# Scores and query projections on two concurrent 64-row PE tiles, one run per two head pairs, values and output projection in 128-row mode

## The chip, the cores and the metric

One core of one Trainium2 chip. The metric is the device time of one execution in microseconds (us), lower is better; the runs of the kernel before in this study lie between 947.7 and 952.4 us. A profile shows one execution. PE is the matrix engine (PEld its weight loads), DVE the vector engine, ACT the engine of the exponentials, POOL and SP the engines whose queues start DMAs here.

## The reference, cut to what matters

```python
x = A_x                                   # 2048 x 640
xn = layernorm(x)
q = xn @ wq                               # 32 heads of 192
k, v = last 512 rows of the caches, per head
s = softmax(q k^T * 192**-0.5) v @ wo     # attention, output projection
h = sigmoid(xn @ w_gate) * (xn @ w_up)
out = x + s * silu(h @ w_down)
```

## The kernel before

The gating part (h, w_down) comes first and takes 168 us. Attention then goes through 8 groups of two head pairs, and in each group through 4 blocks of 512 query rows. A step is one head pair in one block: scores, output projection of an earlier block, query projection of the next step, values. A head has 192 = 128 + 64 contraction rows, so a pair has four full 128-row score matmuls per half of the keys, and 64-row ones that two heads can run at once on the upper and lower half of the PE array:

```python
def stage_q(s, hp):                       # query projection, 128-row mode
    for j in range(PC):                   # 3 tiles of 128 columns per pair
        q_ps = bank()
        for c in range(NCD):              # 5 chunks of 128 rows
            nc.tensor.matmul(q_ps, lhsT=wqp[:, c, j*P:(j+1)*P], rhs=xnT[s][:, c, :], ...)
        # copied to SBUF by ACT (j == 1) or DVE

def full(S_ps, c, i, start):              # 128 rows
    nc.tensor.matmul(S_ps, lhsT=kT[:, c*PC + 2*i, :], rhs=qT[2*i][:], ...)
def half(S_ps, c, i, start):              # 64 rows, head i on half i of the array
    r = slice(64*i, 64*i + 64)
    nc.tensor.matmul(S_ps, lhsT=kT[r, c*PC + 1, :], rhs=qT[1][r, :], ...)

for u in u0: full(*u, True)               # 4 full
for u in u0: half(*u, False)              # 4 half   } one run of eight
for u in u1: half(*u, True)               # 4 half   } in 64-row mode
for u in u1: full(*u, False)              # 4 full
# ... (exponentials by ACT, one per 512 columns)

# a step: scores, two tiles of output projection (stage_wo), stage_q of the next, values
```

Each pair's values are normalised by DVE into o_st and transposed by a DMA into oT, which the output projection reads two steps later.

The softmax here doesn't subtract the row's maximum and nothing guards it: scores larger than these inputs give would overflow.

## Time and profile before

Median 949.78 us; the profiled execution spans 946.2 us. The head of the page of the kernel before: busy time and share of the span per engine, and the granted PE clock in 40 slices.

```profile
span 946.2 us, 16135 instructions
...
PE 933.0 (99%) x6554; PEld 533.6 (56%) x6554; DVE 443.3 (47%) x927; ACT 345.8 (37%) x654; POOL 160.6 (17%) x206
...
PEclk9999999999999999999999999999999999999999
```

The waits of PE in the kernel before (engine and line, what it waited for, us in total, times, longest):

```profile
PE ps_all L219 <- ACT xnT_89 L238: 3.2, 4, 0.8
PE ps_all L208 <- DVE warm L205: 1.5, 1, 1.5
PE ps_all L339 <- DVE qT_1587 L330: 0.6, 1, 0.6
PE ps_all L414 <- DMA oT<-o_st: 0.3, 1, 0.3
```

PE is busy 99% and waits for others for 5.6 us in all, so its time is the sum of the intervals from one matmul's start to the next. A step takes 12.02 us (402.89 to 414.91 below, the same score matmul of two successive steps). The scores of one step, from the timeline (start us, duration us, engine, line, operation, count, idle before):

```profile
402.89 0.38 PE L339 MATMUL ps_all<-qT_3908,kT 128*128 128x512 bf16 x1
...
403.10 0.38 PE L339 MATMUL ps_all<-qT_3922,kT 128*128 128x512 bf16 x1
403.41 0.55 PEld L346 LDWEIGHTS <-kT 64*128 64x128 bf16 x8 [0.42 <-issue]
403.41 1.04 PE L346 MATMUL ps_all<-qT_3915,kT 64*128 64x512 bf16 x8
...
404.38 0.39 PE L339 MATMUL ps_all<-qT_3908,kT 128*128 128x512 bf16 x1
404.61 0.38 PE L339 MATMUL ps_all<-qT_3922,kT 128*128 128x512 bf16 x1
...
414.91 0.38 PE L339 MATMUL ps_all<-qT_4028,kT 128*128 128x512 bf16 x1
```

Read starts, not durations: a 512-column matmul takes 0.38 us but the next starts 0.216 us later. From 403.10 to 403.41, into the 64-row matmuls, it is 0.31; the eight take 0.97 to the next start, where four pairs at 0.216 would take 0.864. That is about 0.2 us per step that moves no data: the two changes of tile mode.

### The profile page before, as it was taken

How to read it: one execution, taken by the hardware profiler on the slowest of the kernel's cores; microseconds unless marked ns; L12 is line 12 of the kernel's file. 1: busy time of each engine (PE TensorE's matmuls, PEld its weight loads, DVE VectorE, ACT ScalarE, POOL GpSimd, SP SyncE). 2: the span in 40 equal slices, each digit the busy share in tenths (PEclk: the TensorE clock that was granted, in tenths of full speed). 3: DMA queues.
4: the chain of work that ended last, by engine and by line, in shares of the span. 5: the costliest groups of instructions: out<-in, count | busy, mean ns of one | idle time of the engine just before them, and what ended most of it. 6: DMA issues, size and time to landing. Idle time of an engine off the chain costs nothing. (4 is left out here: it accounts for less than half of the span.)

```text
span 946.2 us, 16135 instructions
## 1 busy us (share of the span) xinstructions
PE 933.0 (99%) x6554; PEld 533.6 (56%) x6554; DVE 443.3 (47%) x927; ACT 345.8 (37%) x654; POOL 160.6 (17%) x206
## 2 busy tenths in 40 slices
PE   7999999999999999999999999999999999999996
PEld 5445455555555555555555555555555555555554
DVE  4842322444444444444444444444444444444566
ACT  3322222443333333333333333333333333333330
POOL 7100000400200020001100110011001106666100
PEclk9999999999999999999999999999999999999999
DMA  9940000651473157325631463147314833333433
GB/s 292 232 91 29 1 29 15 209 95 31 100 100 84 35 88 114 85 34 88 114 84 34 89 113 84 35 76 126 85 34 56 145 90 82 87 87 88 120 87 103
DMA packets 149258, 84.41 MB, mean 89 GB/s; under 512 B 136480, under 2 KB 139040, under 8 KB 149184
## 3 DMA queue, kind: packets, MB, share of 16 engines
q1 hardware_dynamic: 136384, 36.71, 23.1%
q0 software_dynamic: 12800, 46.67, 18.4%
q8 instruction: 51, 0.84, 0.4%
q14 instruction: 23, 0.19, 0.1%
HBM read 44.70 MB, written 5.24 MB: 53 GB/s over the span
## 5 line engine op out<-in xcount | busy, mean ns | idle before, releaser
L414 PE MATMUL ps_all<-wo_g,oT 128*128 128x512 bf16 (+1 forms) x1536 | 219.0, 299 | 0.3 <-DMA oT<-o_st 0.3
L414 PEld LDWEIGHTS <-oT 128*128 128x128 bf16 x1536 | 120.6, 98 | 98.3 <-DMA oT<-o_st 0.7
L322 PEld LDWEIGHTS <-wqp 128*128 128x128 bf16 x960 | 91.4, 98 | 106.1
L388 DVE TENSOR_TENSOR o_st<-ps_all,rden 128x384 bf16<-128x384 f32 x256 | 142.8, 558 | 8.9
L339 PEld LDWEIGHTS <-kT 128*128 128x128 bf16 x512 | 43.7, 97 | 58.7 <-issue 28.2
L270 DVE TENSOR_TENSOR hT_sb<-ps_all,sig_sb 128x512 bf16<-128x512 f32 x48 | 32.6, 682 | 52.7 <-PE ps_all L264 45.3
L322 PE MATMUL ps_all<-xnT_90,wqp 128*128 128x512 bf16 x240 | 54.4, 379 | 0.0
L322 PE MATMUL ps_all<-xnT_89,wqp 128*128 128x512 bf16 x240 | 54.4, 379 | 0.0
L322 PE MATMUL ps_all<-xnT_91,wqp 128*128 128x512 bf16 x240 | 54.4, 379 | 0.0
L322 PE MATMUL ps_all<-xnT_92,wqp 128*128 128x512 bf16 x240 | 54.4, 379 | 0.0
L279 PE MATMUL ps_all<-wd_sb,hT_sb 128*128 128x512 bf16 (+1 forms) x384 | 52.8, 299 | 0.0
L269 ACT ACTIVATE sig_sb<-ps_all 128x512 bf16<-128x512 f32 x48 | 28.6, 597 | 66.0 <-PE ps_all L264 52.2
L346 PEld LDWEIGHTS <-kT 64*128 64x128 bf16 x512 | 19.6, 94 | 42.4 <-issue 27.1
L387 DVE RECIPROCAL rden<-ps_all 128x2 f32<-128x2 f32 x256 | 41.6, 163 | 3.5
L279 PEld LDWEIGHTS <-hT_sb 128*128 128x128 bf16 x384 | 29.7, 98 | 23.1
L264 PEld LDWEIGHTS <-wu_sb 128*128 128x128 bf16 x225 | 22.0, 98 | 26.5
L264 PEld LDWEIGHTS <-wg_sb 128*128 128x128 bf16 x225 | 21.9, 98 | 26.2 <-issue 0.4
L313 POOL DMA_DIRECT2D wo_g<-in_A_wo_dram x8 | 6.9, 859 | 173.0 <-PE ps_all L414 170.8
L292 POOL DMA_DIRECT2D gB_d<-gB_sb x16 | 8.7, 545 | 128.7 <-DVE gB_sb L287 128.7
L287 DVE TENSOR_TENSOR gB_sb<-ps_all,sg 128x640 bf16<-128x640 f32 x16 | 13.2, 825 | 34.6 <-ACT sg L286 34.6
L128 POOL DMA_DIRECT2D v_sb_93<-in_A_v_cache_dram x4 | 3.0, 749 | 154.3 <-PE ps_all L381 153.5
L128 POOL DMA_DIRECT2D v_sb_101<-in_A_v_cache_dram x4 | 3.0, 749 | 153.2 <-PE ps_all L381 153.2
(924 smaller groups left out, 1527.1 us busy)
## 6 DMA issues: line engine op xcount, KB each, us to landing
wqp<-in_A_wq_dram POOLq DMA_DIRECT2D x16, 480.0 KB, 8.5
wo_g<-in_A_wo_dram POOLq DMA_DIRECT2D x8, 960.0 KB, 5.8
k_sb<-in_A_k_cache_dram POOLq DMA_DIRECT2D x32, 192.0 KB, 5.6
gBa_sb<-gB_d POOLq DMA_DIRECT2D x32, 160.0 KB, 2.7
gB_d<-gB_sb POOLq DMA_DIRECT2D x16, 160.0 KB, 2.1
xa_sb<-in_A_x_dram POOLq DMA_DIRECT2D x16, 160.0 KB, 2.9
out_dram<-o_sb SPq DMA_DIRECT2D x16, 160.0 KB, 2.4
wd_sb<-in_B_w_down_dram POOLq DMA_DIRECT2D x1, 1920.0 KB, 17.1
```

The costliest lines, as they stand in the source:

```text
L264: nc.tensor.matmul(ps, lhsT=w[:, c, f * P:(f + 1) * P], rhs=xnT[s][:, c, :], start=(c == 0), stop=(c == NCD - 1),)
L269: nc.scalar.activation(sig_sb[:], g_ps, AF.Sigmoid)
L270: nc.vector.tensor_tensor(hT_sb[:, f, :], u_ps, sig_sb[:], ALU.mult)
L279: nc.tensor.matmul(oB_ps[:, d0:d0 + dsz], lhsT=hT_sb[:, f, q * P:(q + 1) * P], rhs=wd_sb[:, f, d0:d0 + dsz], start=(f == 0), stop=(f == NF ...
L287: nc.vector.tensor_tensor(gB_sb[:], oB_ps[:, 0:D], sg[:], ALU.mult)
L292: nc.gpsimd.dma_start(gB_d[t * P:(t + 1) * P, :], gB_sb[:])
L322: nc.tensor.matmul(q_ps, lhsT=wqp[:, c, j * P:(j + 1) * P], rhs=xnT[s][:, c, :], start=(c == 0), stop=(c == NCD - 1),)
L339: nc.tensor.matmul(S_ps, lhsT=kT[:, c * PC + 2 * i, :], rhs=qT[2 * i][:], start=start, stop=not start,)
L346: nc.tensor.matmul(S_ps, lhsT=kT[r, c * PC + 1, :], rhs=qT[1][r, :], start=start, stop=not start,)
L387: nc.vector.reciprocal(rden[:], o_ps[:, :, DH:DH + 1])
L388: nc.vector.tensor_tensor(o_st[:, qp * 2:qp * 2 + 2, i * DH:(i + 1) * DH], o_ps[:, :, 0:DH], rden[:].to_broadcast([P, 2, DH]), ALU.mult,)
L414: nc.tensor.matmul(oA[:, d0:d0 + dsz], lhsT=oTs[pp][:, q * PC + j, :], rhs=wo_t[g][:, cc, d0:d0 + dsz], start=(cc == 0), stop=(cc == n - 1),)
```

## The change

Its intent: all scores and the query projections are cut into 64-row pieces that run as pairs on the two halves of the array, for two head pairs of a block in one run of 11.7 us. Values and output projection follow in 128-row mode. So PE changes its mode twice per two head pairs instead of four times. That needs q with a head per half of the partitions, weights of wq in pieces of 64 x 64 columns (six loads per pair with runs of 128 bytes instead of one load with runs of 768 bytes), k in pieces of 64 columns, and a second copy xnS of the transposed x with its halves swapped. PSUM is handed out as four double banks; one exponential covers two banks. The last output tile is finished in two halves of 320 columns.

```diff
-    def bank(): ...                      # eight single banks
+    ring = list(range(4))                # four double banks
+    def bank2():
+        b = ring.pop(0); ring.append(b)
+        return ps_all[:, 2 * b:2 * b + 2, :]
# ... load_pair
-        wqp = wq_pool.tile([P, NCD, 2 * DH], BF16, name="wqp")
-        nc.gpsimd.dma_start(wqp[:], wq_r[:, :, hp * 2 * DH:(hp + 1) * 2 * DH])
+        for j in range(PC):
+            jj = (hp % G) * PC + j
+            r = HI if jj % 2 else LO
+            for i in range(2):
+                d0 = (2 * hp + i) * DH + j * HF
+                nc.gpsimd.dma_start(
+                    wqp[r, jj // 2, :, i, :],
+                    wq_r[:, :, :, d0:d0 + HF].rearrange("p c h n -> p (c h) n"),
+                )
# ... stage_q, per two of a block's six tiles
+        for c in range(NCD):
+            for h in range(2):
+                for b, r in enumerate((LO, HI)):
+                    x = xnT if b == h else xnS
+                    nc.tensor.matmul(
+                        ps[:, b, :], lhsT=wq_t[g][r, u, 2 * c + h].rearrange("p i e -> p (i e)"),
+                        rhs=x[s][r, c, :], ...)
+        nc.vector.tensor_copy(qT_t[n][:, 2 * u:2 * u + 2, :], ps)
# ... stage_s, one chunk of keys of one pair
+        for j in range(PC):
+            for b, r in enumerate((LO, HI)):
+                nc.tensor.matmul(
+                    ps[:, b, :], lhsT=kT[r, c * PC + j, :], rhs=qT[r, pp * PC + j, :], ...)
+        nc.scalar.activation(E_t[n, pp][:, c, :, :], ps, AF.Exp, scale=scale_qk)
# ... the last output tile
+            h = D // 2
+            for d0, d1 in ((0, h), (h, D)):
+                wo_mm(...); finish(oA, gB_sb, t, d0, d1)
# ... the order of a block
+        for k, (pp, c) in enumerate(todo):           # 8 score units
+            stage_s(n, pp, c)
+            if k % 2 == 1 and k // 2 < G * PC // 2 and n < last:
+                stage_q(n + 1, k // 2)               # 3 projection units
+        for k, u in enumerate(pv):                   # 4 value units,
+            stage_pv(*u)                             # an output tile after each
+            stage_wo(*wo[k])
```

More of the change, by code (lines that the diff above doesn't have):

```diff
@@ L55 @@
     NG = NPAIR // G
-    HOLD = 2
     NWARM = 12
@@ L73, with flat @@
     ps_all = psum.tile([P, 8, 512], F32, name="ps_all")
-    ring = list(range(8))
-    def bank():
+    ring = list(range(4))
+    def bank2():
         b = ring.pop(0)
         ring.append(b)
-        return ps_all[:, b, :]
-    def bank2():
-        pos = {b: i for i, b in enumerate(ring)}
-        b = min(range(7), key=lambda b: max(pos[b], pos[b + 1]))
-        for x in (b, b + 1):
-            ring.remove(x)
-            ring.append(x)
-        return ps_all[:, b:b + 2, :].rearrange("p b n -> p (b n)")
+        return ps_all[:, 2 * b:2 * b + 2, :]
+    def flat(ps):
+        return ps.rearrange("p b n -> p (b n)")
     ident = const.tile([P, P], BF16, name="ident")
@@ L98 @@
     xnt_pool = ctx.enter_context(tc.tile_pool(name="xnt_pool", bufs=1, **rs))
-    wq_pool = ctx.enter_context(tc.tile_pool(name="wq_pool", bufs=2 * G, **rs))
+    wq_pool = ctx.enter_context(tc.tile_pool(name="wq_pool", bufs=2, **rs))
     k_pool = ctx.enter_context(tc.tile_pool(name="k_pool", bufs=2, **rs))
@@ L102 @@
     v_pool = ctx.enter_context(tc.tile_pool(name="v_pool", bufs=1, **rs))
+    HF = 64
+    LO, HI = slice(0, HF), slice(HF, P)
+    xnS = [xnt_pool.tile([P, NCD, 512], BF16, name=f"xnS{s}") for s in range(NST)]
     xnT = [xnt_pool.tile([P, NCD, 512], BF16, name=f"xnT{s}") for s in range(NST)]
@@ L111 @@
         v_tiles.append(vt)
-    wq_r = A_wq.rearrange("(c p) n -> p c n", p=P)
+    wq_r = A_wq.rearrange("(c h p) n -> p c h n", h=2, p=HF)
     wo_r = A_wo.rearrange("(c p) d -> p c d", p=P)
@@ L118, in load_pair @@
     def load_pair(hp):
-        k_sb = k_pool.tile([P, KC, 2, DH], BF16, name="k_sb")
+        k_sb = k_pool.tile([P, KC * PC, 2, 64], BF16, name="k_sb")
         vv = []
@@ L124, in load_pair @@
                 k_sb[:, :, i, :],
-                A_k_cache[0, hk, Sk - W:Sk, :].rearrange("(p j) d -> p j d", j=KC),
+                A_k_cache[0, hk, Sk - W:Sk, :].rearrange("(p k) (j e) -> p (k j) e", k=KC, j=PC),
             )
@@ L133, in load_pair @@
         v_t[hp] = vv
-        wqp = wq_pool.tile([P, NCD, 2 * DH], BF16, name="wqp")
-        nc.gpsimd.dma_start(wqp[:], wq_r[:, :, hp * 2 * DH:(hp + 1) * 2 * DH])
-        wq_t[hp] = wqp
+        if hp % G == 0:
+            wq_t[hp // G] = wq_pool.tile([P, G * PC // 2, NCD * 2, 2, HF], BF16, name="wqp")
+        wqp = wq_t[hp // G]
+        for j in range(PC):
[7 more added lines that the diff above has]
+                )
         kT = kt_pool.tile([P, KC * PC, P], BF16, name="kT")
-        nc.sync.dma_start_transpose(kT[:], k_sb[:].rearrange("p j e d -> p (j e d)"))
+        nc.sync.dma_start_transpose(kT[:], k_sb[:].rearrange("p k i e -> p (k i e)"))
         kT_t[hp] = kT
@@ L205 @@
         nc.vector.memset(warm[:], 0.0)
-        w_ps = bank()
+        pT_banks = bank2()
+        w_ps = pT_banks[:, 0, :]
         for _ in range(NWARM):
             nc.tensor.matmul(w_ps, lhsT=warm[:, 0:P], rhs=warm[:], start=True, stop=True)
-        gu_first = [
-            [bank() for _ in range(2)] for _ in range(FA)
-        ]
+        gu_first = [bank2() for _ in range(FA)]
         def first_mm(q, f):
             r = slice(q * P, (q + 1) * P)
-            for ps, w in zip(gu_first[f], (wg_sb, wu_sb)):
+            for i, w in enumerate((wg_sb, wu_sb)):
                 for c in range(NCD):
                     nc.tensor.matmul(
-                        ps[:, r], lhsT=w[:, c, f * P:(f + 1) * P], rhs=xnT[0][:, c, r],
+                        gu_first[f][:, i, r], lhsT=w[:, c, f * P:(f + 1) * P], rhs=xnT[0][:, c, r],
                         start=(c == 0), stop=(c == NCD - 1),
                     )
-        pT_banks = [w_ps, bank()]
         ln_stats(0)
@@ L234 @@
             xn = ln_apply(q)
-            pT = pT_banks[q % 2][:, 0:NCD * P // 2].bitcast(BF16).rearrange("p (c n) -> p c n", c=NCD)
+            pT = pT_banks[:, q % 2, 0:NCD * P // 2].bitcast(BF16).rearrange("p (c n) -> p c n", c=NCD)
             for c in range(NCD):
@@ L258 @@
                 if s == 0 and f < FA:
-                    g_ps, u_ps = gu_first[f]
+                    gu = gu_first[f]
                 else:
-                    g_ps, u_ps = bank(), bank()
-                    for ps, w in ((g_ps, wg_sb), (u_ps, wu_sb)):
+                    gu = bank2()
+                    for i, w in enumerate((wg_sb, wu_sb)):
                         for c in range(NCD):
                             nc.tensor.matmul(
-                                ps, lhsT=w[:, c, f * P:(f + 1) * P], rhs=xnT[s][:, c, :],
+                                gu[:, i, :], lhsT=w[:, c, f * P:(f + 1) * P], rhs=xnT[s][:, c, :],
                                 start=(c == 0), stop=(c == NCD - 1),
@@ L268 @@
                 sig_sb = bwork.tile([P, 512], BF16, name="sig_sb")
-                nc.scalar.activation(sig_sb[:], g_ps, AF.Sigmoid)
-                nc.vector.tensor_tensor(hT_sb[:, f, :], u_ps, sig_sb[:], ALU.mult)
+                nc.scalar.activation(sig_sb[:], gu[:, 0, :], AF.Sigmoid)
+                nc.vector.tensor_tensor(hT_sb[:, f, :], gu[:, 1, :], sig_sb[:], ALU.mult)
                 if s == 0 and TQ + f < NST * TQ:
@@ L275 @@
             for q in range(TQ):
-                oB_ps = bank2()
+                oB_ps = flat(bank2())
                 for f in range(NF):
@@ L292 @@
                 nc.gpsimd.dma_start(gB_d[t * P:(t + 1) * P, :], gB_sb[:])
+            if s == 0:
+                for ss in range(NST):
+                    nc.sync.dma_start(xnS[ss][LO], xnT[ss][HI])
+                    nc.sync.dma_start(xnS[ss][HI], xnT[ss][LO])
     acc_pool = ctx.enter_context(tc.tile_pool(name="acc_pool", bufs=1))
@@ L298 @@
     e_pool = ctx.enter_context(tc.tile_pool(name="e_pool", bufs=2))
-    ost_pool = ctx.enter_context(tc.tile_pool(name="ost_pool", bufs=3))
-    oT_pool = ctx.enter_context(tc.tile_pool(name="oT_pool", bufs=3 * G))
+    ost_pool = ctx.enter_context(tc.tile_pool(name="ost_pool", bufs=2))
+    oT_pool = ctx.enter_context(tc.tile_pool(name="oT_pool", bufs=2 * G))
     small = ctx.enter_context(tc.tile_pool(name="small", bufs=8))
@@ L314, in load_group, with stage_q @@
         wo_t[g] = wo_g
-    def stage_q(s, hp):
-        wqp = wq_t[hp]
-        qT = []
+    def stage_q(n, u):
+        g, s = blocks[n]
+        if u == 0:
+            qT_t[n] = qT_pool.tile([P, G * PC, 512], BF16, name="qT")
+        ps = bank2()
+        for c in range(NCD):
[4 more added lines that the diff above has]
+                        ps[:, b, :], lhsT=wq_t[g][r, u, 2 * c + h].rearrange("p i e -> p (i e)"),
+                        rhs=x[s][r, c, :],
+                        start=(c == 0 and h == 0), stop=(c == NCD - 1 and h == 1),
+                    )
+        nc.vector.tensor_copy(qT_t[n][:, 2 * u:2 * u + 2, :], ps)
@@ L319, in stage_q, with stage_s @@
+    def stage_s(n, pp, c):
+        g, s = blocks[n]
+        kT, qT = kT_t[g * G + pp], qT_t[n]
+        if c == 0:
+            E_t[n, pp] = e_pool.tile([P, KC, 2, 512], BF16, name="E")
+        ps = bank2()
         for j in range(PC):
-            q_ps = bank()
-            for c in range(NCD):
+            for b, r in enumerate((LO, HI)):
                 nc.tensor.matmul(
-                    q_ps, lhsT=wqp[:, c, j * P:(j + 1) * P], rhs=xnT[s][:, c, :],
-                    start=(c == 0), stop=(c == NCD - 1),
-                )
@@ L326, in stage_q @@
-            qT_sb = qT_pool.tile([P, 512], BF16, name=f"qT{j}", tag=f"qT{j}")
-            if j == 1:
-                nc.scalar.activation(qT_sb[:], q_ps, AF.Copy)
-            else:
-                nc.vector.tensor_copy(qT_sb[:], q_ps)
-            qT.append(qT_sb)
-        return qT
-    def stage_s(hp, qT):
-        kT = kT_t[hp]
-        E = [e_pool.tile([P, KC, 512], BF16, name=f"E{i}", tag=f"E{i}") for i in range(2)]
-        def full(S_ps, c, i, start):
-            nc.tensor.matmul(
-                S_ps, lhsT=kT[:, c * PC + 2 * i, :], rhs=qT[2 * i][:],
-                start=start, stop=not start,
-            )
-        def half(S_ps, c, i, start):
-            r = slice(64 * i, 64 * i + 64)
-            nc.tensor.matmul(
-                S_ps, lhsT=kT[r, c * PC + 1, :], rhs=qT[1][r, :],
-                start=start, stop=not start,
-            )
-        def units(cs):
-            return [(bank(), c, i) for c in cs for i in range(2)]
-        def exps(us):
-            for S_ps, c, i in us:
-                nc.scalar.activation(E[i][:, c, :], S_ps, AF.Exp, scale=scale_qk)
-        u0 = units(range(0, KC // 2))
-        for u in u0:
-            full(*u, True)
-        for u in u0:
-            half(*u, False)
-        exps(u0)
-        u1 = units(range(KC // 2, KC))
-        for u in u1:
-            half(*u, True)
-        for u in u1:
-            full(*u, False)
-        exps(u1)
-        return E
@@ L372, in stage_pv @@
-    def stage_pv(hp, E):
-        o_st = ost_pool.tile([P, TQ, 2 * DH], BF16, name="o_st")
-        for i in range(2):
-            vt = v_t[hp][i]
-            for qp in range(TQ // 2):
-                o_ps = bank()[:, 0:2 * OW].rearrange("p (i n) -> p i n", i=2)
-                for ii in range(2):
-                    q = qp * 2 + ii
-                    for c in range(KC):
-                        nc.tensor.matmul(
-                            o_ps[:, ii, 0:DH + 1], lhsT=E[i][:, c, q * P:(q + 1) * P],
-                            rhs=vt[:, c, 0:DH + 1],
-                            start=(c == 0), stop=(c == KC - 1),
-                        )
-                rden = small.tile([P, 2, 1], F32, name="rden")
-                nc.vector.reciprocal(rden[:], o_ps[:, :, DH:DH + 1])
-                nc.vector.tensor_tensor(
-                    o_st[:, qp * 2:qp * 2 + 2, i * DH:(i + 1) * DH],
-                    o_ps[:, :, 0:DH], rden[:].to_broadcast([P, 2, DH]), ALU.mult,
-                )
-        oT = oT_pool.tile([P, TQ * PC, P], BF16, name="oT")
-        nc.sync.dma_start_transpose(oT[:], o_st[:].rearrange("p q d -> p (q d)"))
-        return oT
+                    ps[:, b, :], lhsT=kT[r, c * PC + j, :], rhs=qT[r, pp * PC + j, :],
@@ new lines, in stage_s, with stage_pv @@
+                    start=(j == 0), stop=(j == PC - 1),
+                )
+        nc.scalar.activation(E_t[n, pp][:, c, :, :], ps, AF.Exp, scale=scale_qk)
+    def stage_pv(n, pp, i):
+        g, s = blocks[n]
+        hp = g * G + pp
+        if i == 0:
+            ost_t[0] = ost_pool.tile([P, TQ, 2 * DH], BF16, name="o_st")
+        o_st = ost_t[0]
+        E, vt = E_t[n, pp], v_t[hp][i]
+        o_ps = bank2()[:, :, 0:2 * OW].rearrange("p b (i n) -> p b i n", i=2)
+        for q in range(TQ):
+            for c in range(KC):
+                nc.tensor.matmul(
+                    o_ps[:, q // 2, q % 2, 0:DH + 1], lhsT=E[:, c, i, q * P:(q + 1) * P],
+                    rhs=vt[:, c, 0:DH + 1],
+                    start=(c == 0), stop=(c == KC - 1),
+                )
+        rden = small.tile([P, 2, 2, 1], F32, name="rden")
+        nc.vector.reciprocal(rden[:], o_ps[:, :, :, DH:DH + 1])
+        nc.vector.tensor_tensor(
+            o_st[:, :, i * DH:(i + 1) * DH].rearrange("p (b i) d -> p b i d", b=2),
+            o_ps[:, :, :, 0:DH], rden[:].to_broadcast([P, 2, 2, DH]), ALU.mult,
+        )
+        if i == 1:
+            oT = oT_pool.tile([P, TQ * PC, P], BF16, name="oT")
+            nc.sync.dma_start_transpose(oT[:], o_st[:].rearrange("p q d -> p (q d)"))
+            oT_t[n, pp] = oT
@@ L407, in prep_last, with wo_mm, finish, stage_wo @@
         nc.gpsimd.tensor_tensor(acc[t][:], acc[t][:], x_sb[:], ALU.add)
-    def wo_mm(oA, g, oTs, q, ccs):
-        n = G * PC
-        for cc in ccs:
+    def wo_mm(oA, n, q, d_ch):
+        g, s = blocks[n]
+        nn = G * PC
+        for cc in range(nn):
             pp, j = divmod(cc, PC)
-            for d0, dsz in d_chunks:
+            for d0, dsz in d_ch:
                 nc.tensor.matmul(
-                    oA[:, d0:d0 + dsz], lhsT=oTs[pp][:, q * PC + j, :], rhs=wo_t[g][:, cc, d0:d0 + dsz],
-                    start=(cc == 0), stop=(cc == n - 1),
-                )
-    def wo_out(oA, g, s, q, gB_sb):
-        t = s * TQ + q
-        if g == NG - 1:
-            t_sb = fin.tile([P, D], F32, name="t_sb")
-            o_sb = fin.tile([P, D], BF16, name="o_sb")
-            nc.vector.tensor_tensor(t_sb[:], oA[:, 0:D], gB_sb[:], ALU.mult)
-            nc.vector.tensor_tensor(o_sb[:], t_sb[:], acc[t][:], ALU.add)
-            nc.sync.dma_start(of[t * P:(t + 1) * P, :], o_sb[:])
+                    oA[:, d0:d0 + dsz], lhsT=oT_t[n, pp][:, q * PC + j, :],
+                    rhs=wo_t[g][:, cc, d0:d0 + dsz],
+                    start=(cc == 0), stop=(cc == nn - 1),
+                )
+    def finish(oA, gB_sb, t, d0, d1):
+        t_sb = fin.tile([P, D], F32, name="t_sb")
+        o_sb = fin.tile([P, D], BF16, name="o_sb")
+        d = slice(d0, d1)
+        nc.vector.tensor_tensor(t_sb[:, d], oA[:, d], gB_sb[:, d], ALU.mult)
+        nc.vector.tensor_tensor(o_sb[:, d], t_sb[:, d], acc[t][:, d], ALU.add)
+        nc.sync.dma_start(of[t * P:(t + 1) * P, d], o_sb[:, d])
+    def stage_wo(n, q):
+        g, s = blocks[n]
+        t = s * TQ + q
+        gB_sb = load_gate(t) if g == NG - 1 else None
+        oA = flat(bank2())
+        if n == len(blocks) - 1 and q == TQ - 1:
+            h = D // 2
+            for d0, d1 in ((0, h), (h, D)):
+                wo_mm(oA, n, q, [
+                    (max(d0, a), min(d1, a + b) - max(d0, a))
+                    for a, b in d_chunks if max(d0, a) < min(d1, a + b)
+                ])
+                finish(oA, gB_sb, t, d0, d1)
+            return
+        wo_mm(oA, n, q, d_chunks)
+        if g == NG - 1:
+            finish(oA, gB_sb, t, 0, D)
         elif g == 0:
@@ L432, in wo_out @@
             prep_last(t)
-    def stage_wo(g, s, oTs, q):
-        gB_sb = load_gate(s * TQ + q) if g == NG - 1 else None
-        oA = bank2()
-        wo_mm(oA, g, oTs, q, range(G * PC))
-        wo_out(oA, g, s, q, gB_sb)
-    steps = [
-        (g, s, hp) for g in range(NG) for s in range(NST) for hp in range(g * G, (g + 1) * G)
-    ]
-    wo_queue = []
-    oT_of = {}
-    load_group(0)
-    qT = stage_q(steps[0][1], steps[0][2])
-    for k, (g, s, hp) in enumerate(steps):
-        if s == 0 and hp == g * G and g + 1 < NG:
-            load_group(g + 1)
-        E = stage_s(hp, qT)
-        keep = max(0, k + HOLD + 1 - len(steps))
-        for _ in range(TQ // G):
-            if len(wo_queue) > keep and wo_queue[0][0] <= k:
-                stage_wo(*wo_queue.pop(0)[1:])
-        if k + 1 < len(steps):
-            qT = stage_q(steps[k + 1][1], steps[k + 1][2])
-        oT_of[hp] = stage_pv(hp, E)
-        if hp == g * G + G - 1:
-            oTs = [oT_of[h] for h in range(g * G, (g + 1) * G)]
-            for q in range(TQ):
-                wo_queue.append((k + 2, g, s, oTs, q))
@@ L463 @@
-    tail = wo_queue[-TQ:]
-    for w in wo_queue[:-TQ]:
-        stage_wo(*w[1:])
-    gBs = [load_gate(s * TQ + q) for _, _, s, _, q in tail]
-    oAs = [bank2() for _ in tail]
-    n = G * PC
-    for oA, (_, g, s, oTs, q) in zip(oAs, tail):
-        wo_mm(oA, g, oTs, q, range(0, n - PC))
-    for oA, gB_sb, (_, g, s, oTs, q) in zip(oAs, gBs, tail):
-        wo_mm(oA, g, oTs, q, range(n - PC, n))
-        wo_out(oA, g, s, q, gB_sb)
+    blocks = [(g, s) for g in range(NG) for s in range(NST)]
@@ new lines @@
+    qT_t, E_t, oT_t, ost_t = {}, {}, {}, {}
+    load_group(0)
+    for u in range(G * PC // 2):
+        stage_q(0, u)
+    last = len(blocks) - 1
+    for n, (g, s) in enumerate(blocks):
+        if s == 0 and g + 1 < NG:
+            load_group(g + 1)
+        todo = [(pp, c) for pp in range(G) for c in range(KC)]
+        for k, (pp, c) in enumerate(todo):
+            stage_s(n, pp, c)
+            if k % 2 == 1 and k // 2 < G * PC // 2 and n < last:
+                stage_q(n + 1, k // 2)
+        pv = [(n, pp, i) for pp in range(G) for i in range(2)]
+        wo = [(n - 1, q) for q in range(TQ)] if n > 0 else []
+        if n < last:
+            for k, u in enumerate(pv):
+                stage_pv(*u)
+                if wo:
+                    stage_wo(*wo[k])
+        else:
+            for k, u in enumerate(pv):
+                stage_pv(*u)
+                if k == 1:
+                    stage_wo(*wo.pop(0))
+            for u in wo:
+                stage_wo(*u)
@@ L477 @@
+    for q in range(TQ):
+        stage_wo(last, q)
 _INS = ['A_x', 'A_k_cache', 'A_v_cache', 'A_wq', 'A_wo', 'B_x', 'B_w_gate', 'B_w_up', 'B_w_down']
```

## The prediction

> **What bounds it now.** TensorE. The page gives PE 99% busy; between 200 and 925 us it is busy throughout at full clock; the list of PE's waits holds 5.6 us, nearly all at the start. DVE (47%), ACT (37%) and DMA (42%) have room. So the time is the sum of PE's issue intervals. The timeline shows one step (one head pair, one 512-row block) every 12.02 us, 64 steps: scores 2.79, output projection 3.26 (216 and 56 ns start to start), query projection 3.24 (15 x 216 ns), values 2.73 (32 x 85 ns).
>
> Only scores miss their streaming rate. Four 128-row matmuls, eight 64-row ones in four concurrent pairs and four 128-row ones are worth 12 x 216 = 2.59 us, not 2.79. Going into the pairs, the interval is 311 ns instead of 216, the next 227; coming out 309, then 225. So one change of tile mode costs about 104 ns; 128 of them 13.3 us. The Trainium skill, "TensorEngine Tiling (Array Packing)", Key Properties, says that changing the mode drains the engine; the trace agrees. Within the eight, the two of a pair start 2 to 4 ns apart and pairs come every 216 ns, each with its own weights: two 64-row tiles lose nothing.
>
> **What the change does.** PE's streaming is the same: per two head pairs, 24 score pairs (5.18 us), 30 projection pairs (6.48), values (5.46) and output projection (6.52), 23.64 us, plus two mode changes (0.21) = 23.85, against 24.04. That saves 0.21 us in each of 32 blocks: 6.7 us, all on the critical path. Instructions grow by about 960 load/matmul pairs, but four per 216 ns is 54 ns each, easier than the 43 ns that the values stage sustains.
>
> Off the path: exponentials become 128x1024 (estimate 0.9 us each from the 0.48 us spacing of two 512s; 8 in an 11.7 us run); q copies all go to DVE (1.2 us by doubling, 3 per run); normalisation takes 768 columns at a time. With four double banks I find every buffer free before PE wants it. oT has about 14 us from its last value to its first use; it needs about 6.5. wq comes as 128-byte pieces in six DMAs per pair; DMA and POOL have room.
>
> Start of attention: the 0.57 us wait for qT goes. End: before, values end at about 928.3 and the kernel 18 us later, with six output tiles left. After, seven tiles are left and PE stalls about 1.6 us for the last transpose, but the last tile is finished in halves, so the end after the last matmul shrinks from 7.6 to about 4.3 us: net gain about 2 us.
>
> **Sum:** 949.8 - 6.7 - 0.5 - 2 = 940.6 us. Range 937 to 947. Faster by over 2%: 3%; within 2%: 93%; slower: 4%.
>
> **What would show it.** PE still 99%; block period 23.85 us in the timeline; 64-row pairs every 216 ns through runs of 11.7 us; two intervals with about 95 ns extra per block; no PE waits for ACT, DVE or oT mid-kernel; a short wait for oT near the end.
>
> **What would make it wrong.** 64-row pairs slower than 216 ns over long runs, or the two projection streams (xnT and swapped copy) not starting together: 10 ns per pair costs 17 us. A mode change before values costing more than 104 ns. Late xnT transposes near 50 us, if the kT transposes ahead of them wait for k behind the many wq DMAs. oT late where new kT loads share its queue. PE waiting on double banks.

## The result and the profile after

Median 943.71 us (942.26 to 944.12) against 948.9 us; ratio 0.994, interval 0.9917 to 0.9962. By the 2% rule that is "same"; it is a gain of 5 us where 9 were predicted. The head of the page of the changed kernel, then PE's waits:

```profile
span 942.4 us, 18325 instructions
...
PE 926.7 (98%) x8032; PEld 540.3 (57%) x8032; DVE 450.3 (48%) x641; ACT 298.5 (32%) x334; POOL 224.6 (24%) x286
...
PEclk9999999999999999999999999999999999999999
```

```profile
PE ps_all L410 <- DVE t_sb L420: 4.2, 1, 4.2
PE ps_all L229 <- ACT xnT_93 L247: 3.2, 4, 0.8
PE ps_all L410 <- DMA oT<-o_st: 2.1, 2, 1.9
PE ps_all L219 <- DVE warm L215: 1.5, 1, 1.5
PE ps_all L273 <- DVE xn L207: 0.5, 1, 0.5
```

Three waits are new: 4.2 us for DVE, 2.1 for oT, 0.5 in the gating stage. The run itself, in PE's timeline of the changed kernel (L359 scores, L343 projection, L410 output projection, L375 values):

```profile
406.90 0.43 PE L410 MATMUL ps_all<-wo_g,oT 128*128 128x512 bf16 x2
407.27 1.47 PE L359 MATMUL ps_all<-qT,kT 64*128 64x512 bf16 x12
408.57 0.38 PE L343 MATMUL ps_all<-xnT_96,wqp 64*128 64x512 bf16 x1
408.58 0.59 PE L343 MATMUL ps_all<-xnS_92,wqp 64*128 64x512 bf16 x2
...
417.64 1.46 PE L359 MATMUL ps_all<-qT,kT 64*128 64x512 bf16 x12
419.03 1.53 PE L375 MATMUL ps_all<-v_sb_97,E 128*128 128x193 bf16 x16
```

Twelve 64-row matmuls in six pairs start 1.30 us before the next (407.27 to 408.57, 6 x 0.216), and the projection from xnT and from xnS starts together. From the last scores at 417.64 to the values at 419.03 it is 1.39, 0.09 more than six pairs. In the trace's single starts, the interval at the entries is 152 ns instead of 56 (median), at the exits 308 instead of 216 (471 in the last block, where PE waits for an exponential), and the first interval after it some 10 ns longer. In the profiled execution 28 of the 30 block periods after the first are 23.83 us, against 24.04 for two steps before.

Where the profiled 3.8 us (946.2 to 942.4) come from, by starts of matmuls. (The medians differ by 5.2; the profiled run of the changed kernel, 944.12 us, was the slowest of its four.) Gating: the first projection starts at 168.62 instead of 167.83, 0.8 us later. From there to the last values matmul: 753.75 us instead of 760.34, 6.6 less; one output tile (1.63 us) that was inside is now behind, and waits for oT of 0.4 and 2.0 us were added. From there to the end: 20.0 us instead of 18.0, 1.6 of which is that tile. So the rhythm gave what was foreseen, and the start of gating, late oT and the tail took about half of it.

The tail of the changed kernel, in DVE's and then PE's timeline (L420 and L421 finish a tile, o_sb is what leaves):

```profile
927.59 0.82 DVE L420 TENSOR_TENSOR t_sb<-ps_all,gBa_sb 128x640 f32<-128x640 f32 x1
929.34 0.83 DVE L421 TENSOR_TENSOR o_sb<-t_sb,acc_1582 128x640 bf16<-128x640 f32 x1 [0.94 <-DMA out_dram<-o_sb]
930.08 0.82 DVE L420 TENSOR_TENSOR t_sb<-ps_all,gBa_sb 128x640 f32<-128x640 f32 x1
932.78 0.83 DVE L421 TENSOR_TENSOR o_sb<-t_sb,acc_1583 128x640 bf16<-128x640 f32 x1 [1.88 <-DMA out_dram<-o_sb]
...
936.83 0.48 DVE L420 TENSOR_TENSOR t_sb<-ps_all,gBa_sb 128x320 f32<-128x320 f32 x1
```

```profile
922.45 10.76 PE L410 MATMUL ps_all<-wo_g,oT 128*128 128x512 bf16 x78
937.36 0.99 PE L410 MATMUL ps_all<-wo_g,oT 128*128 128x192 bf16 x12 [4.16 <-DVE t_sb L420]
```

DVE twice waits for an output row block that is still on its way, because o_sb has two buffers. PE has done six and a half of seven tiles by 933.2 and then waits 4.16 us with the second half of the last one until DVE has read the first half at 936.83.

The late oT: POOL's and then SP's queue of the changed kernel around the start of the fourth group. The 12 loads of wq and those of k and v start just when the last oT of the old group (the second of the two) is transposed.

```profile
448.43 4.30 POOL L143 DMA_DIRECT2D wqp<-in_A_wq_dram  x6
...
456.98 4.30 POOL L143 DMA_DIRECT2D wqp<-in_A_wq_dram  x6
```

```profile
448.74 7.51 SPq L388 DMA_TRANSPOSE oT<-o_st  x2
456.36 14.98 SPq L148 DMA_TRANSPOSE kT<-k_sb  x2
```

```profile
DMA to landing us min/median/max: 3.6/3.8/16.2
```

That last line is oT's from issue to landing in the changed kernel: 3.8 us as a rule, but 8.5 to 16.2 for the last oT of a group (from the second group's loads on), while the output projection that reads it starts 13.4 us after its issue. The same line of the kernel before:

```profile
DMA to landing us min/median/max: 3.6/3.7/12.9
```

There the last oT of a group took 8.1 to 12.5 us, with 13.7 us until its output projection (the 12.9 is that of the other pair, which had a step more). So the slack was nearly used up already, and the trace that the prediction was made from shows it.

### The profile page after: what moved, and what is told of

Same layout as the page of the kernel before. It is cut to its first block, busy times and chain, and to the rows that moved or that the text cites. A ratio compares the mean times of both kernels' runs of the same rounds, so it can differ in the third digit from the quotient of the medians.

```text
span 942.4 us, 18325 instructions
## 1 busy us (share of the span) xinstructions
PE 926.7 (98%) x8032; PEld 540.3 (57%) x8032; DVE 450.3 (48%) x641; ACT 298.5 (32%) x334; POOL 224.6 (24%) x286
## 3 DMA queue, kind: packets, MB, share of 16 engines
q0 software_dynamic: 15360, 46.68, 22.6%
## 5 line engine op out<-in xcount | busy, mean ns | idle before, releaser
L363 ACT ACTIVATE E<-ps_all 128x1024 bf16<-128x1024 f32 x256 | 248.1, 1023 | 498.4 <-PE ps_all L359 451.5
L410 PE MATMUL ps_all<-wo_g,oT 128*128 128x512 bf16 (+2 forms) x1542 | 228.8, 298 | 6.3 <-DVE t_sb L420 4.2
L348 DVE CAST qT<-ps_all 128x1024 bf16<-128x1024 f32 x96 | 117.6, 1225 | 225.4 <-PE ps_all L343 225.4
L359 PE MATMUL ps_all<-qT,kT 64*128 64x512 bf16 x1536 | 186.7, 376 | 0.0
L375 PEld LDWEIGHTS <-E 128*128 128x128 bf16 x2048 | 171.0, 98 | 24.4 <-issue 13.6
L410 PEld LDWEIGHTS <-oT 128*128 128x128 bf16 x1542 | 121.6, 97 | 82.9 <-issue 4.4
L343 PEld LDWEIGHTS <-wqp 64*128 64x128 bf16 x1920 | 93.4, 94 | 113.8 <-issue 0.3
L359 PEld LDWEIGHTS <-kT 64*128 64x128 bf16 x1536 | 72.3, 94 | 91.8 <-issue 7.3
L382 DVE TENSOR_TENSOR o_st<-ps_all,rden 128x768 bf16<-128x768 f32 x128 | 122.6, 958 | 4.7 <-DVE rden L381 0.2
L143 POOL DMA_DIRECT2D wqp<-in_A_wq_dram x96 | 68.9, 728 | 13.2 <-DMA wd_sb<-in_B_w_down_dram 5.4
L343 PE MATMUL ps_all<-xnT_95,wqp 64*128 64x512 bf16 x240 | 55.7, 376 | 0.0
L343 PE MATMUL ps_all<-xnT_96,wqp 64*128 64x512 bf16 x240 | 55.7, 376 | 0.0
L343 PE MATMUL ps_all<-xnT_94,wqp 64*128 64x512 bf16 x240 | 55.7, 376 | 0.0
L343 PE MATMUL ps_all<-xnS_92,wqp 64*128 64x512 bf16 x240 | 55.6, 376 | 0.0
L343 PE MATMUL ps_all<-xnS_91,wqp 64*128 64x512 bf16 x240 | 55.6, 376 | 0.0
L343 PE MATMUL ps_all<-xnS_90,wqp 64*128 64x512 bf16 x240 | 55.6, 376 | 0.0
L343 PE MATMUL ps_all<-xnT_93,wqp 64*128 64x512 bf16 x240 | 55.4, 376 | 0.0
L343 PE MATMUL ps_all<-xnS_89,wqp 64*128 64x512 bf16 x240 | 55.3, 376 | 0.0
```

What stands on the lines that cost most here:

```text
L143: nc.gpsimd.dma_start(wqp[r, jj // 2, :, i, :], wq_r[:, :, :, d0:d0 + HF].rearrange("p c h n -> p (c h) n"),)
L343: nc.tensor.matmul(ps[:, b, :], lhsT=wq_t[g][r, u, 2 * c + h].rearrange("p i e -> p (i e)"), rhs=x[s][r, c, :], start=(c == 0 and h == 0), ...
L348: nc.vector.tensor_copy(qT_t[n][:, 2 * u:2 * u + 2, :], ps)
L359: nc.tensor.matmul(ps[:, b, :], lhsT=kT[r, c * PC + j, :], rhs=qT[r, pp * PC + j, :], start=(j == 0), stop=(j == PC - 1),)
L363: nc.scalar.activation(E_t[n, pp][:, c, :, :], ps, AF.Exp, scale=scale_qk)
L375: nc.tensor.matmul(o_ps[:, q // 2, q % 2, 0:DH + 1], lhsT=E[:, c, i, q * P:(q + 1) * P], rhs=vt[:, c, 0:DH + 1], start=(c == 0), stop=(c = ...
```

## The experiments

Eleven variants and a control, four to a job (the runs of one job share their rounds and chip; the three jobs were on three chips). All passed the comparison with the reference, e5 too, which has its projection weights in the wrong places: so that comparison hardly sees the scores, and says little of the query path. The others keep the changed kernel's query path, but for e3, whose weight order is mine.

### The control

The changed kernel unchanged, on the chip of the next three.

> Control: the changed kernel again, on the same chip as the three others. Expected 943.5 us, blocks of 23.83 us, and again a PE wait of some 4 us for DVE in the last tile. Open: whether the PE wait of 1.9 us for oT at the start of the fourth group of heads is in every execution or only in the one profiled.

Median 946.1 us (944.25 to 950.9), ratio to before 0.997 (0.9956 to 0.9984). The kernel before stayed at 948.7. So the changed kernel itself varies by more than its gain. PE's waits in this profile, and its clock in three slices (window, its length, PE, PEld, DVE, ACT and POOL busy, clock, DMA share, GB/s):

```profile
PE ps_all L410 <- DMA oT<-o_st: 4.3, 3, 2.1
PE ps_all L410 <- DVE t_sb L420: 4.0, 1, 4.0
...
PE ps_all L273 <- DMA xnT<-xn: 2.6, 1, 2.6
```

```profile
660.00:664.00 4.00, 3.86 (x37) 2.32 (x34) 1.99 (x3) 1.94 (x2) 0.00 (x0) 1.00 1.14 112
664.00:668.00 4.00, 1.94 (x11) 1.31 (x12) 0.87 (x2) 0.00 (x0) 0.00 (x0) 0.81 1.21 188
668.00:672.00 4.00, 4.00 (x31) 3.16 (x30) 1.70 (x4) 0.00 (x0) 0.00 (x0) 0.76 0.02 5
```

The wait in the tail is the same; that for oT is there again, longer and at another group start as well, and PE waits for xnT in the gating stage. One gap of 2.3 us before 666 was followed by about 3.4 us at half clock: values matmuls then start every 161 ns instead of 86, and that block took 27.79 us = 23.83 + 2.31 + 1.65. The 2.0 us gap in the first profile had no such sequel, nor had one of 2.5 us in e1; one of 3.1 us in e7 had.

### More changes of mode

One (e1) or two (e2) of a block's output tiles are moved from the values stage into the middle of the next 64-row run.

```diff
             if k % 2 == 1 and k // 2 < G * PC // 2 and n < last:
                 stage_q(n + 1, k // 2)
+            if k in (3, 5) and late:
+                stage_wo(*late.pop(0))
# ... in the values stage
+            late = wo[TQ - 1:]           # TQ - 2 in e2
+            wo = wo[:TQ - 1]
```

> One output projection tile per block is moved from the values stage into the middle of the next block's 64-row run, so that 30 blocks have two more changes of tile mode and nothing else. Theory (a change of mode costs 0.104 us of PE time, and the gain of the change is the number of changes saved): 30 x 0.208 = 6.2 us slower than the changed kernel, blocks of 24.04 us, about 949.7 us. Rival (the gain comes from the merged banks and the longer exponentials, mode changes cost nothing net): same time as the changed kernel, 943.5 us.

> Two output projection tiles per block moved into the 64-row run at two places: four more changes of mode per block. Theory: 12.5 us slower than the changed kernel, blocks of 24.25 us, about 956 us, twice the step of the first. Rival: 943.5 us.

Measured: 952.05 us (ratio 1.004) and 957.75 us (1.0097) against the control's 946.1: 5.95 and 11.65 us slower, for 6.2 and 12.5 expected. The trace counts 64 mode changes in the control, 124 and 184 here. The starts of two successive runs of the changed kernel, then of e1:

```profile
383.44 1.47 PE L359 MATMUL ps_all<-qT,kT 64*128 64x512 bf16 x12
...
407.27 1.47 PE L359 MATMUL ps_all<-qT,kT 64*128 64x512 bf16 x12
```

```profile
411.64 1.47 PE L359 MATMUL ps_all<-qT,kT 64*128 64x512 bf16 x12
...
435.68 1.47 PE L359 MATMUL ps_all<-qT,kT 64*128 64x512 bf16 x12
```

23.83 against 24.04 us, and 24.25 in e2: 0.21 us for each two changes, in a straight line. The rival, that only merged banks and longer exponentials count, is out: e1 and e2 keep both. The block periods carry this verdict, since the times also hold each kernel's late transposes.

### Projection in 128-row mode after the score run

```diff
-        for c in range(NCD):
-            for h in range(2):
-                for b, r in enumerate((LO, HI)):
-                    # 64-row pairs from xnT and xnS
+        for b in range(2):
+            for c in range(NCD):
+                nc.tensor.matmul(ps[:, b, :], lhsT=wq_t[g][:, 2*u + b, c]..., rhs=xnT[s][:, c, :], ...)
# ... and stage_q after all eight stage_s instead of between them
```

> Scores in one 64-row run of eight, then the query projections in 128-row mode (weights in the order of columns that they need, loaded in as many pieces of 128 bytes, without the swapped copy's use): as many changes of mode as the changed kernel. Theory: without projections between them, eight score units take 5.2 us on PE and their exponentials about 7.5 us on ACT, and the four double banks run out; in the last block of the changed kernel, which has no projections, this already cost 0.35 us. So 31 x 0.35 = 10.9 us slower, about 954 us, with PE waits for ACT in the list of waits. Rival (64-row projections cost something themselves, and what counts is only the number of mode changes): same as the changed kernel or faster.

Measured: 951.7 us (1.0028), 5.6 slower than the control, not 10.9. Two successive runs start at

```profile
435.55 5.56 PE L352 MATMUL ps_all<-qT,kT 64*128 64x512 bf16 x48
...
459.73 1.47 PE L352 MATMUL ps_all<-qT,kT 64*128 64x512 bf16 x12
```

24.18 us apart, 0.35 more than 23.83: exactly the term expected, in every block. In the single starts it sits in two places: 405 ns before the last score unit and 468 ns before the first projection, where 216 and 309 are the rule. That is where PE needs a double bank whose exponential is not yet done: the exponentials of these two banks end at 440.23 and 441.15 us, and the matmuls start 0.05 us later. My expectation that the list of waits would show it was wrong: a matmul's modelled duration of 0.38 us covers gaps this short. The total fell short of 31 x 0.35 because this kernel lost less elsewhere: 0.4 us to oT and 1.2 to xnT in its profile, against 4.3 and 2.6 in the control's, and no lapse of the clock (one profile each, and the control's is its slowest run). Why its oT came sooner (10.8 us at the longest) I did not settle; its wq loads have as many pieces of 128 bytes, but write all 128 partitions where the changed kernel's write 64. So with four double banks the projections belong in the run as well: between score units they give ACT its time.

### What makes oT late

e4 issues the wq loads of a group one and a half blocks earlier, apart from k and v:

```diff
+            if s in (1, 2):              # in the gating stage: first two groups
+                load_wq(s - 1)
# ...
+        if s == 3 and g + 2 < NG:
+            load_wq(g + 2)
         if s == 0 and g + 1 < NG:
             load_group(g + 1)            # k, v and wo, as before
```

> The wq loads of a group are issued a block and a half earlier, apart from the k and v loads (and those of the first two groups later in the gating stage). Theory (wq in pieces of 128 bytes, together with k and v, fills the DMA engines just when the last oT of a group is transposed, which lands after 8 to 16 us instead of 3.7, and delays the first xnT transposes): oT landings at the group starts at most 8 us, no PE wait for oT in the middle, no wait near 51 us; 2 to 3 us less than the changed kernel, about 941 us. Rival (the order of the transposes in their queue, kT before oT, is the cause): landings and waits as in the changed kernel, same time.

e5 leaves the loads where they are, but takes wq in one load per pair with runs of 768 bytes; its weights are in wrong places.

```diff
-        # six loads, runs of 128 bytes
+        nc.gpsimd.dma_start(wqp_flat[...], wq_128rows[:, :, hp*2*DH:(hp+1)*2*DH])
```

> WRONG RESULT ON PURPOSE: wq is loaded at the same place and with the same bytes, but one load per pair in pieces of 768 bytes as before the change, so the projections see weights in the wrong places. Theory (it is the number of pieces): software DMA share falls from 22.6% to about 20%, oT landings at group starts at most 9 us, no PE wait for oT in mid-kernel, about 941 us. Rival (the bytes or the k pieces are the cause): landings still up to 12 or 16 us.

Measured: e4 942.92 us (0.9931; 941.65 to 943.78), e5 941.79 us (0.9919; 941.08 to 942.23). The control's ratio was 0.997, and its runs spread over 6.6 us where these spread over 2.1 and 1.1. But the changed kernel's first ratio was 0.994, from which e4 and e5 do not differ clearly; what can be compared are e6 and e7 below, of the same rounds and with late oT (0.9953 and 0.9951), and the landings. The landing of oT in e4, then in e5 (3.6/3.8/16.2 in the changed kernel):

```profile
DMA to landing us min/median/max: 3.6/4.2/8.6
```

```profile
DMA to landing us min/median/max: 3.6/3.7/10.2
```

Neither list of PE's waits has oT or a DMA for xnT any more. The share of the software DMA queue is 20.1% in e4 and 18.9% in e5, 22.6% in the changed kernel, with the same bytes. The rival of e4, kT before oT in the queue, is out by the trace of the changed kernel itself: its oT that took 16.2 us was issued at 454.7 us, before the kT of 456.4, and so it is at every group start but the first. The rival of e5 is out too: it has the bytes and the k pieces of the changed kernel, and still no oT that PE waits for. So it is the form of the wq loads. Which trait of it is open: e5 has larger pieces, one load instead of six, and writes all partitions at once; and e3, with as many small pieces in as many loads, has an oT of 10.8 us at the longest, nearly that of e5. So the number of small pieces alone does not make it late. e4 shows that the same loads do little harm one and a half blocks earlier. The Trainium skill, "DMA: Bandwidth & Descriptors", Specifications, gives 512 bytes as the least size for line rate; e5 fits that, with 3.7 points less of the queue's share for larger pieces, but e4 has 2.5 points less with the small ones, by issuing them at another time. Both came out 1 to 2 us above my figures, and e5's 10.2 missed "at most 9".

### The tail

e6: four buffers for o_sb. e7: last tile in one piece.

```diff
-        o_sb = fin.tile(...)             # bufs=2
+        o_sb = osb_pool.tile(...)        # bufs=4         (e6)
-        if n == len(blocks) - 1 and q == TQ - 1:   # halves
+        if False:                                  #       (e7)
```

> Four buffers instead of two for o_sb, the finished rows on their way out. Theory: DVE waits 2.8 us in the tail for outputs still in flight; without it DVE's chain is 2.8 us earlier, PE's wait for DVE in the last tile falls from 4.2 to about 1.4 us, and the kernel ends 2.8 us earlier, about 940.7 us. Rival (DVE is simply the slower engine of the tail, the DMA wait is hidden): under 1 us.

> The last tile's output projection in one piece, not in two halves that share a PSUM bank. Theory (the second half waits for DVE to read the first half out of the same bank, and DVE comes late anyway, so the split only adds): PE's wait of 4.2 us for DVE is gone, PE ends near 933.7 us, but DVE still ends its chain near 938.5 us; 0.5 to 1 us faster than the changed kernel, about 943 us. Rival (the split pays, as intended, by starting the last evacuation early): 0.5 to 1 us slower.

Measured: 945.05 us (0.9953) and 945.2 us (0.9951), with spreads of 6.2 and 4.3 us: inconclusive as times, since late oT cost their profiles 6.1 and 3.1 us of PE waits. The waits moved as expected: in e6 DVE no longer waits for outputs and PE waits 1.5 us for DVE instead of 4.2; in e7 PE's wait for DVE is gone. So I repeated both on top of early wq, where that noise is small.

> Early wq loads with four o_sb buffers, the tail fix measured where no transpose comes late. Theory (DVE in the tail waits 2.7 to 2.8 us for outputs in flight, and everything after hangs on DVE): 2.7 us less than with early wq alone, about 940.2 us; PE's last wait for DVE 1.5 us instead of 4. Rival (DVE's wait is hidden): same as early wq alone, 942.9 us.

> Early wq loads, and the last tile cut at column 512, the bank boundary, instead of at 320. Theory (the second half waits because it writes the bank that DVE has yet to read): the 4 us wait of PE for DVE is gone although DVE is just as late; the end moves little, because DVE has still 1.65 us per tile to do: 0 to 0.7 us less than early wq alone. Rival (PE waits for DVE for another reason, such as a free double bank): the wait stays at about 4 us.

> All three: early wq loads, four o_sb buffers, last tile in one piece. Theory (the losses found are the whole of what was missing): 3.5 us less than early wq alone, about 939.3 us, which is under the 940.6 us that was predicted for the change; no PE wait over 0.5 us after the first 20 us. If it stays above 941 us, something else is missing.

> As the one before, with the last tile cut at the bank boundary instead of whole. Theory (with DVE the later engine at the end, a cut gains nothing and adds two instructions): within 0.5 us of the whole tile. Rival (the cut lets evacuation start early, as intended): 0.5 to 1 us faster than the whole tile.

| early wq plus | median us | range | ratio to before |
|---|---|---|---|
| nothing (e4, other job) | 942.92 | 941.65 to 943.78 | 0.9931 |
| four o_sb buffers (e8) | 938.57 | 937.72 to 940.04 | 0.9890 |
| cut at 512 (e9) | 941.91 | 939.83 to 943.87 | 0.9921 |
| four buffers, whole (e10) | 938.62 | 937.59 to 941.95 | 0.9895 |
| four buffers, cut at 512 (e11) | 938.55 | 937.77 to 939.38 | 0.9887 |

By the medians, four buffers give 3.3 us (e8 against e9 of the same rounds) or 4.4 (against e4, another job), and the three with four buffers lie within 0.1 us. But these runs spread over 1.6 to 4.4 us, and e9's profiled run lost about 3 us to half clock near its start, so the tails in the traces say more: from the start of the last values matmul to the end of the execution, one profile each.

| tail, us | cut at 320 | cut at 512 | whole |
|---|---|---|---|
| two o_sb buffers | 20.0 (changed kernel), 20.6 (control), 20.6 (e4), 20.9 (e5) | 19.7 (e9) | 19.1 (e7) |
| four o_sb buffers | 17.3 (e6), 17.3 (e8) | 16.6 (e11) | 16.3 (e10) |

Four buffers give 2.7 to 3.3 us with every cut, which is what DVE waited for outputs: most of the lost time of the tail. Against the other cuts, the one at 320 adds another 0.7 to 1.1 us with four buffers and 0.3 to 1.8 with two, as e7 expected and against its rival; the medians are too coarse to show it. That PE's wait comes from the cut inside a bank, e9 shows. Its waits of PE hold no DVE after the first microseconds, although DVE still waits for outputs and is as late as ever:

```profile
DVE o_sb L426 <- DMA out_dram<-o_sb: 3.3, 3, 2.0
```

A cut at 320 puts the second half into the bank that DVE has yet to read, a cut at 512 does not. This agrees with the Trainium skill, "PSUM — Partial Sum Buffer", PSUM bank collisions raise a hardware error, which says that two engines must not touch one bank of the same partitions at a time and that a compiler orders all such accesses; here 4.0 us in e4 became none in e9. That wait cost much less than its length, since DVE was the later engine; in the control, e4 and e5 the last matmuls after it also ran at half clock (160 ns where the changed kernel has 82). PE's waits in e10, complete:

```profile
PE ps_all L232 <- ACT xnT L250: 3.2, 4, 0.8
PE ps_all L222 <- DVE warm L218: 1.4, 1, 1.4
PE ps_all L232 <- DMA wu_sb<-in_B_w_up_dram: 0.2, 1, 0.2
```

After the first 20 us nothing of note is left in e10. In e8 and e11 PE waits once more for DVE, 0.9 us for o_st near 884 us; that was not followed up. With 938.6 us e8, e10 and e11 beat both kernels, the one before by 10 us and the changed one by 5 to 7.5 us, as its median is 943.7 or 946.1 (other jobs); e10 was the simplest.

## Why the prediction was right or wrong

The time, 943.7 us, lies in the range of 937 to 947, and it is "same" as foreseen. The gain was about half of the predicted one. That the time still fell in the range owes something to its width, and to a start from 949.78 us, 0.9 above the later median: for the profiled pair the same terms give 946.2 - 9.2 = 937.0 us, 5.4 below the measured 942.4. All three errors, below, went the same way.

- "One change of tile mode costs about 104 ns", 0.21 us per block, 6.7 us in all: right. Block period 23.83 us for 23.85 predicted; e1 and e2 add 0.21 us per two changes.
- "64-row pairs every 216 ns" through runs of 11.7 us, with the two projection streams together: right, from the starts.
- "Four double banks ... every buffer free before PE wants it": right in the run; e3 shows how close it is, since without projections between score units the same banks cost 0.35 us per block.
- "The 0.57 us wait for qT goes": right; the first score starts when the projections end.
- "oT has about 14 us ... it needs about 6.5" and "DMA and POOL have room": this step failed at the starts of groups, where oT needed up to 16.2 us. Even the trace of the kernel before had 8.1 to 12.5 us there, not 6.5. The mean share of DMA (42%) said nothing of that stretch, where it was full (the trace's share is 1.1 to 1.2 from 450 to 470 us). It was named as a risk, with the shared queue as the cause; e5 shows that it is the form of the wq loads, and which trait of it stays open. Cost 2.4 us in the first profile, more in the control, and there once another 1.65 us of lower clock.
- The gating stage was named as a risk too (late xnT transposes), and cost 0.8 us in the first profile.
- "Net gain about 2 us" at the end: wrong in sign. The tail took 20.0 us from the last values, not the 17.6 that the step implies; with the tile that moved behind, 0.4 us more than before. The end after the last matmul did shrink as foreseen, from 7.5 to 4.0 us, but that matmul came later. I foresaw a 1.6 us stall for oT (in the tail there was none over 0.25), and not that DVE, with two o_sb buffers, would wait 2.8 us for outputs, nor that the second half of the last tile shares a bank with the first. The tails of e6 to e11 show both: the first costs about 3 us, the second 0.7 to 1.1 where four buffers have taken the first away.
- "About 960" more load/matmul pairs: 1478, since scores grow too. It did not matter.

The sum, with the measured terms of the profiled pair: 946.2 - 6.7 - 0.6 + 0.8 + 2.4 + 0.4 = 942.5; the span was 942.4.

## What to carry to other kernels

Where PE is busy 99%, compare the starts of successive matmuls with the streaming interval: a change of tile mode shows as about 0.1 us at its border, and is worth counting per block. A change that only reorders a full engine gave its count here, and lost half of it again in places that it did not aim at: check each load whose form it changes against the slack at the moment it is issued, by the longest landing in the trace and not by the median or the mean share, and follow the tail to the last buffer. When a kernel's runs spread by several us, judge by block periods and by the length of stages in the trace, and remove the spread before measuring anything smaller.

## What the Trainium skill lacked or had wrong

- "TensorEngine Tiling (Array Packing)", Key Properties: says that a change of mode drains PE, but not at what price. Here 0.104 us of PE time per change (about 95 ns at the border and 10 after it), the same in both directions and for 64, 124 and 184 changes.
- "TensorE: Matmul & The Clock Gate", Why this matters for your kernels: asks for no gaps over about 3 us. Here a gap of 2.3 us was once followed by 3.4 us at half clock (161 ns instead of 86 between values matmuls), one of 2.0 and one of 2.5 us (e1) were not.
- "DMA: Bandwidth & Descriptors", Specifications: states the 512 bytes there, not what small pieces do to transfers beside them. Here DMA transposes beside six loads in pieces of 128 bytes landed after up to 16.2 us (median 3.8), and after up to 10.2 when the same bytes came in one load in pieces of 768; other traits of the loads differ too (e3: pieces of 128 bytes, 10.8).
- "PSUM — Partial Sum Buffer", PSUM bank collisions raise a hardware error: does not say what the ordering of accesses to one bank costs. Here cutting a tile inside a bank made a wait of 4 us and about 1 us of tail, cutting it at the bank's edge no wait.
